# DeltaNet attention and a top-2 expert layer on one Trainium2 core: indirect stores tied to the matmul plan, early tiles in two passes, and another layout of the diagonal copies

## Chip, cores and metric

The kernel runs on one NeuronCore of a Trainium2 chip. The metric is device time in microseconds for the whole kernel. The kernel before took 837.7 us (median of 3 runs, 837.05 to 840.62). All arithmetic is in fp32.

## The reference

```python
# attention: q, k, v are [4, 8, 768, 48], beta is [4, 8, 768]
k_n = k / (norm(k) + 1e-6)
for t in range(768):
    y[:, :, t] = q_t @ state                       # [48] @ [48, 48] per batch and head
    state += beta_t * outer(k_t, v_t - k_t @ state)
x = y laid out as [3072 tokens, 384]
# router and experts: E = 8 experts, D = 384, F = 1024
noisy = x @ w_gate + log1p(exp(x @ w_noise)) * noise
top2, with weights softmax over the two
out[token] += weight_e * relu(x[token] @ w1[e]) @ w2[e]   # for both of its experts
```

## The kernel before

**Attention phase.** The recurrence is done in chunks of 64 tokens. A *unit* is one chunk of two batches (128 partitions) with all 8 heads; four units make a *step* of 128 tokens per batch, and there are six steps (0 to 5), 24 units. For each unit, `products` transposes the keys on TensorE, multiplies them with themselves into two PSUM banks (a `pair` tile), and copies the 32x32 diagonal blocks into an "inverse" tile `t` (four copies of 32 partitions x 256 elements, L658) and the off-diagonal blocks into `at` (L665). `invert` turns a group of one or two steps (`GROUPS`) into inverses on VectorE: a 32x32 transpose (L713), then 30 columns of two operations each (L773, L777), then transposes back (`turn_back`, L793 to L808). `join` builds the 64x64 inverse from the 32x32 ones (L836 copies, L856 and L862 matmuls of 32x32). `recur` scales v on GpSimd (L900), subtracts the state's part on VectorE (L926), solves (L963), and updates the state; `answer` writes the tokens' outputs y (L1044), transposes them and computes the router's logits (L1060). Tiles of y form a ring of three (`NY = 3`), so step 5 uses the tile of step 2.

**Router runs.** `ROUTES` groups the steps in three router runs of two steps. `route` finds the two experts of every token of its 8 units, counts positions with matmuls against a triangular mask, and stores each token's row (384 values of y and 4 of bookkeeping) into the DRAM table `rows_x`, at the slot of each of its two experts: 16 indirect stores of 128 rows per run, issued by GpSimd (`spread`, L396). `cut` raises expert 0's count to a multiple of 128 rows after a step in `EARLY`, so that the tiles before it are complete.

**Early tiles.** `early(s)` computes tiles of expert 0 from rows that are already stored, with weights loaded during the attention phase, in buffers borrowed from the keys of steps 3 and 4 and from q: it loads the rows (L1296), transposes them (L1324), multiplies by w1 (L1350), applies ReLU (L1361), multiplies by w2 (L1374), scales (L1391) and stores them to the output by an indirect DMA (L437). Its jobs have the lowest priority. The kernel before does four tiles at once, after step 3.

**Planner.** All attention-phase work is added to `Jobs`, a list scheduler that runs when the program is built. Every job has an engine, an assumed cost, dependencies (through keys it reads and writes), a due time (`BEGINS`, `ENDS`, `ROUTED`, `STORED`) and perhaps `apart`, a least distance from the last job that has one. `order` simulates the engines: among the jobs of an engine that can begin within `PATIENCE` of the earliest, it takes the one that is due first; a job whose accumulator bank is opened becomes due within `SOON`. The simulated order becomes the order of instructions on each engine; GpSimd's instructions are chained in it. The distance `apart` is not itself in the program: on the chip a store goes as soon as GpSimd reaches it and its inputs are there.

**Expert phase.** After the attention phase the remaining rows of expert 0 are done (`rest`, L1753 and L1765), and experts 1 to 7 follow with a planned sequence of products (L1609).

Of the kernel before, what the change touches and what calls it, by code (L numbers as in the profile page):

```python
# [17 lines left out]
C = 64  # L18
# [1 line left out]
Q = 32  # L20
TILES = 6
MORE = 64
EARLY = {3: (0, 4)}
ROWS = TILES * 128 + MORE
ROW = 384 + 4

# [3 lines left out]
KEYS_AT = [0, 1, 3, 2, 0, 1]  # L30


BEGINS = [37.4, 35.9, 114.1, 181.8]
ENDS = [16.5, 121.4, 125.6, 180.3, 223.6, 257.7]
ROUTED = [145.6, 211.6, 324.9]
STORED = [183.2, 270.8, 339.6]
SOON = 2.12
COLD = [1.6, 1.3, 1.1, 1.1, 1.1, 1.05]
COLD_KEYS = [1.6, 1.6, 1.45, 1.3, 1.1, 1.1]

# [58 lines left out]
class Jobs:  # L99
# [123 lines left out]
                    could[jobs[j].engine].add(j)  # L223
        return sorted(done, key=lambda job: job.start)

    PATIENCE = 0.007

    def run(self, link):

# [11 lines left out]
def kernel(  # L241
# [39 lines left out]
    nc = tc.nc  # L281
# [110 lines left out]
            in_=empty[0:p, None, :].to_broadcast([p, (hi - lo) // p, ROW]),  # L392
        ).ins

    def spread(rows, slot, cleared):
        d = nc.gpsimd.indirect_dma_start(  # L396
            out=rows_x,
            out_offset=bass.IndirectOffsetOnAxis(ap=slot, axis=0),
            in_=rows,
            in_offset=None,  # L400
        ).ins
        tc.declare_no_dep(d, group="spread", reason="no two tokens have the same row")
        tc.add_to_no_dep_group("spread", d)
        for i in cleared:
            tc.add_manual_dep(d, i.name, SYNC, reason="rows cleared before they are written")
        written.append(d)
        return d

# [34 lines left out]
    def deltanet(ictx):  # L443
# [8 lines left out]
        )  # L452
        p_st = psum.tile([128, 2, 512], FP32, name="p_st")
        PE, ACT, DVE, POOL, SP = Jobs.ENGINES

        def bank(size, ahead=False):

# [141 lines left out]
        def turned(n, name, src, slot, to):  # L599

            p = bank(1, True)

            def emit():
                p_t = p.tile.rearrange("p (j t) -> p j t", t=128)
                for j in range(NP):
                    nc.tensor.transpose(p_t[:, j], src(n)[:, 2 * j : 2 * j + 2], ident)

            jobs.add(
                PE, 0.67, emit, reads=halves(name, slot), opens=p,
            )  # L610
            jobs.add(
                ACT, 0.6,
                lambda: nc.scalar.copy(
                    to(n),
                    p.tile.rearrange("p (j t) -> p j t", t=128) if name == "k"
                    else p.tile.rearrange("p (j b t) -> p j b t", b=2, t=C),
                ),
                writes=[(name + "T", slot)], closes=p,
            )

        def by_token(out, lhsT, rhs):

            for j in range(NP):
                for b in range(2):
                    for z in range(2):
                        nc.tensor.matmul(  # L626
                            out[rows_of[b], z, j], lhsT[rows_of[z], j, rows_of[b]],
                            rhs(rows_of[z], j, b), start=(j == 0), stop=(j == NP - 1),
                            skip_group_check=True,
                        )  # L630

        def products(n):

            s, i = divmod(n, US)
            turned(n, "k", kps, slot_of(n), kTs)
            p = bank(2, s > 0)
            jobs.add(  # L640
                PE, 0.69,
                lambda: by_token(
                    two_banks(p, C), kTs(n), lambda z, j, b: kTs(n)[z, j, rows_of[b]]
                ),
                reads=[("kT", slot_of(n))], opens=p,
            )
            _, held_in, half = place_of[s]
            gd = inverses[held_in][:, half].rearrange(
                "p i (u j z) -> p u z j i", u=US, z=2
            )[:, i]  # L650
            for x, lo in enumerate(range(0, 128, Q)):
                rows, cols = slice(lo, lo + Q), slice(lo % C, lo % C + Q)
                on, copy = (DVE, nc.vector.tensor_copy) if s == 0 and x % 2 else (
                    ACT, nc.scalar.copy
                )
                jobs.add(
                    on, 0.38,
                    lambda rows=rows, cols=cols, copy=copy: copy(  # L658
                        gd[rows], two_banks(p, C)[rows, :, :, cols]
                    ),  # L660
                    reads=[("free", held_in, half)], writes=[("gd", held_in, half, i, lo)],
                    uses=p,
                )
            jobs.add(
                ACT, 0.38, lambda: nc.scalar.copy(ats(n), two_banks(p, C)[:, :, :, Q:C]),  # L665
                writes=[("at", slot_of(n))], closes=p,
            )
# [148 lines left out]
        def join(units):  # L816
# [24 lines left out]
            for n, m in zip([*units, None], [None, *units]):  # L841
# [10 lines left out]
                def products_of(n=n, m=m, p_x=p_x):  # L852
                    for h in range(H):
                        for up, dn in pairs:
                            if n is not None:
                                nc.tensor.matmul(  # L856
                                    p_x()[dn, h], ats(n)[up, h % 2, h // 2],
                                    part_of(tbs, n)[up, h], start=(h == 0),
                                    stop=(h == H - 1), skip_group_check=True,
                                )  # L860
                            if m is not None:
                                nc.tensor.matmul(  # L862
                                    p_x()[up, h], xs(m)[dn, h], w64s(m)[dn, h, Q:C],
                                    start=(h == 0), stop=(h == H - 1),
                                    skip_group_check=True,
                                )
# [22 lines left out]
        def recur(n):  # L889
# [50 lines left out]
            if c:  # L940
                p_y = bank(2)

                def of_state():
                    for j in range(NP):
                        for b in range(2):
                            for y in range(2):
                                nc.tensor.matmul(
                                    two_banks(p_y, D)[rows_of[b], y, j],
                                    qss(n)[rows_of[y], j, b, 0:C],
                                    qss(n)[rows_of[y], j, b, C : C + D],  # L950
                                    start=(j == 0), stop=False, skip_group_check=True,
                                )

                jobs.add(
                    PE, 0.68, of_state, reads=[("qT", n % NQ), ("st", n % NQ)],
                    writes=[("of_state", z)], opens=p_y,
                )
            p_u = bank(1)

            def solve():  # L960
                for h in range(H):
                    for b in rows_of:
                        nc.tensor.matmul(  # L963
                            per_head(p_u)[b, h], w64[b, h], v_n[b, h],
                            start=(h == 0), stop=(h == H - 1), skip_group_check=True,
                        )
# [14 lines left out]
            def gather_state():  # L981
                for j in range(NP):
                    for y in range(2):
                        for b in range(2):
                            nc.tensor.matmul(
                                kept[rows_of[y], b, j],
                                kp[rows_of[b], 2 * j + y], u_n[rows_of[b], 2 * j + y],
                                start=(n == 0 and j == 0), stop=(j == NP - 1),
# [14 lines left out]
        def answer(n, p_y):  # L1003
# [11 lines left out]
            def of_chunk():  # L1015
                for j in range(NP):
                    for y in range(2):
                        for b in rows_of:
                            nc.tensor.matmul(  # L1019
                                two_banks(p_y, D)[b, y, j], qk[b, y, j], u_n[b, 2 * j + y],  # L1020
                                start=(c == 0 and j == 0), stop=(j == NP - 1),
                                skip_group_check=True,
# [2 lines left out]
            def turn():  # L1025
                for t in range(KT):
                    cols = slice(t * 128, (t + 1) * 128)
                    nc.tensor.transpose(p_xt.tile[:, cols], y_n[:, cols], ident)  # L1028

            def multiply():  # L1030
                p_l = p_xt.tile[:, KT * 128 : KT * 128 + 2 * E]
                for do in range(KT):
                    nc.tensor.matmul(  # L1033
                        p_l, xTs(n)[:, do], router["wgn"][:, do],
                        start=(do == 0), stop=(do == KT - 1),
                    )
# [44 lines left out]
        def route(g):  # L1081
# [62 lines left out]

            def count_earlier():
                p_at = p.tile[:, 0 : units * E].rearrange("p (u e) -> p u e", e=E)
                nc.tensor.matmul(p_at, mask_u, taken, start=True, stop=False)
                for i in range(1, units):
                    nc.tensor.matmul(
                        p_at[:, i:], ones, taken[:, 0 : units - i],  # L1150
                        start=False, stop=False, skip_group_check=True,
                    )
                nc.tensor.matmul(
                    p_at, ones, before[:, None, :].to_broadcast([128, units, E]),
                    start=False, stop=True,
                )
# [76 lines left out]
            for x in range(units):  # L1233
                of, i = first_s + x // US, x % US
                for to in slot:
# [2 lines left out]
                        lambda x=x, of=of, i=i, to=to: [spread(  # L1238
                            ys(of)[:, i], to[:, x : x + 1],
                            [y for name in clears for y in cleared[name]],  # L1240
                        )],
                        reads=[("slot", g % 2), ("of_y", of % NY), ("y", of % NY, i), *clears],
                        writes=[("rows", of, i, to is slot[1])], lands=2.0, moves=0.7,
                        due=STORED[g], apart=4.5 / steps * paced,
                    )

        def cut(s, rows):
# [4 lines left out]
            def skip():  # L1252
# [7 lines left out]
                )  # L1260

            jobs.add(
                PE, 0.4, lambda: nc.tensor.matmul(p.tile[:, 0:1], ones, before[:, 0:1]),
                reads=["before"], opens=p,
            )
            jobs.add(DVE, 0.4, skip, writes=["before"], closes=p,
# [733 lines left out]
```

## Time and profile before

| | |
|---|---|
| median of 3 runs | 837.7 us |
| the profiled execution's own time | 836.19 us |
| its span, first to last instruction | 834.4 us |
| mean granted clock of TensorE | 0.935 |
| TensorE (PE) matmuls busy | 731.2 us, 88% of the span |
| VectorE (DVE) busy | 555.3 us, 67% |
| ScalarE (ACT) busy | 335.5 us, 40% |
| GpSimd (POOL) busy | 363.8 us, 44% |

Times in the profile count from the first instruction. L396 is line 396 of the kernel; PE, DVE, ACT, POOL and SP are the five engines, PEld is TensorE's loading of weights. In a timeline row the first number is the start, the second how long the merged instructions took; in brackets stands how long the engine was idle before and what ended that. "issue" means that the engine waited for nothing that the profile shows.

### The profile page before, as it was taken

The numbers are of one execution on the slowest core, as the hardware profiler recorded it, in microseconds if no ns is written. First come the engines' busy times: TensorE is split into PE (matmuls) and PEld (weight loads), VectorE is DVE, ScalarE is ACT, GpSimd is POOL, SyncE is SP. The second block draws the span as 40 slices with busy tenths as digits, with TensorE's granted clock in tenths as the row PEclk, the third lists the DMA queues.
The fourth block names the chain that finished last, engine by engine and source line by source line (L and its number), as shares of the span: only waits on it lengthen the run. The fifth ranks groups of instructions, "written<-read, shape, count | busy, mean of one in ns | idle before, by whom it ended". The sixth has DMA issues, their size and how long they took to land.

```text
span 834.4 us, 20583 instructions
## 1 busy us (share of the span) xinstructions
PE 731.2 (88%) x8550; PEld 562.3 (67%) x8550; DVE 555.3 (67%) x1130; ACT 335.5 (40%) x732; POOL 363.8 (44%) x375
## 2 busy tenths in 40 slices
PE   4677778784788678999999999999999999999994
PEld 3456667673677557746558859759669678587593
DVE  5867969990786302205879678688688597796751
ACT  4788689463765225411152051150340430521500
POOL 2111101125300440074457478577675784884511
PEclk9999958985898769999999999999999999999998
DMA  3769855414631331436640921824616407401201
GB/s 58 142 122 324 186 159 118 116 23 137 180 91 39 101 103 52 152 135 139 139 150 1 255 74 40 233 57 87 206 36 174 145 6 196 133 7 54 60 30 33
DMA packets 142215, 93.68 MB, mean 112 GB/s; under 512 B 115868, under 2 KB 134585, under 8 KB 141088
## 3 DMA queue, kind: packets, MB, share of 16 engines
q1 hardware_dynamic: 130448, 64.54, 31.1%
q0 software_dynamic: 9552, 27.33, 9.9%
q8 instruction: 69, 1.13, 0.6%
q10 hardware_dynamic: 2112, 0.39, 0.3%
q14 instruction: 34, 0.28, 0.1%
HBM read 58.82 MB, written 34.81 MB: 112 GB/s over the span
## 4 chain that ended last, share of the span: by engine, by line
PE 53%; issue 5%; POOL 2%; ACT 0%; POOLq 0%; ACTq 0%
PE inner L1609 25%; PE outer L1609 15%; PE pair L1350 3%; PE pair L1374 2%; PE inner L1732 2%; PE inner L1753 2%; PE outer L1765 1%; POOL out_dram L437 1%; POOL sums L428 1%; PE single L1033 1%; PE pair L1019 1%; POOL t_w L1582 0%; PE single L963 0%; PE single L1028 0%; PE pair L626 0%
## 5 line engine op out<-in xcount | busy, mean ns | idle before, releaser
L1692 ACT ACTIVATE hT<-inner 128x416 f32<-128x416 f32 x105 | 54.3, 517 | 256.8 <-PE inner L1609 248.4
L1686 DVE TENSOR_TENSOR hT<-hT,inner 128x416 f32<-128x416 f32 x182 | 105.1, 586 | 45.4 <-PE inner L1609 34.5
L437 POOL DMA_INDIRECT out_dram<-sums,index x52 | 52.9, 1018 | 114.0 <-DVE sums L1512 97.5
L900 POOL TENSOR_TENSOR v<-v,norms 128x384 f32<-128x384 f32 x24 | 21.8, 914 | 164.8 <-DMA v<-in_v_dram 50.3
L1609 PE MATMUL inner<-s_x,w1e 128*128 128x416 f32 x196 | 78.8, 512 | 0.0
L1512 DVE SCALAR_TENSOR_TENSOR sums<-outer,gate,sums 128x192 f32<-128x192 f32 (+1 forms) x113 | 45.8, 415 | 36.1 <-PE outer L1609 35.0
L1681 ACT ACTIVATE hT<-hT 128x416 f32<-128x416 f32 x112 | 60.7, 548 | 21.8 <-DVE hT L1686 13.6
L428 POOL DMA_INDIRECT sums<-out_dram,index x49 | 51.8, 1057 | 19.1 <-issue 11.8
L926 DVE TENSOR_TENSOR v<-v,pair 128x384 f32<-128x384 f32 x22 | 12.1, 552 | 70.9 <-PE pair L626 39.8
L1609 PEld LDWEIGHTS inner<-s_x,w1e 128*128 128x128 f32 x196 | 36.9, 190 | 31.6 <-issue 27.7
L1609 PE MATMUL outer<-t_w,hT 128*128 128x192 f32 x336 | 58.0, 326 | 0.0
L658 ACT COPY t<-pair 32x256 f32<-32x256 f32 x88 | 51.9, 590 | 15.0 <-PE pair L626 9.0
L773 DVE TENSOR_TENSOR part<-t 128x168 f32<-128x168 f32 (+28 forms) x120 | 55.4, 461 | 3.7
L777 DVE TENSOR_TENSOR t<-t,part 128x168 f32<-128x168 f32 (+28 forms) x120 | 54.3, 452 | 4.1
L1609 PE MATMUL inner<-s_x,s_w 128*128 128x416 f32 x140 | 56.9, 512 | 0.0
L396 POOL DMA_INDIRECT rows_x<-y,slot x48 | 48.1, 1002 | 18.9 <-issue 12.4
L1609 PE MATMUL inner<-xe,w1e 128*128 128x416 f32 x140 | 55.8, 513 | 0.0
L1609 PEld LDWEIGHTS outer<-t_w,hT 128*128 128x128 f32 x336 | 55.2, 190 | 0.0
L1566 POOL TENSOR_TENSOR w1e<-w1e 128x256 f32<-128x256 f32 x54 | 51.4, 961 | 2.0
L1609 PE MATMUL outer<-w2e,hT 128*128 128x192 f32 x280 | 50.1, 326 | 0.0
L1609 PEld LDWEIGHTS outer<-w2e,hT 128*128 128x128 f32 x280 | 46.5, 190 | 2.2 <-issue 2.2
L1609 PEld LDWEIGHTS inner<-s_x,s_w 128*128 128x128 f32 x140 | 26.6, 190 | 22.3 <-issue 22.1
(215 smaller groups left out, 1576.0 us busy)
## 6 DMA issues: line engine op xcount, KB each, us to landing
w2e<-in_moe_w_dram SPq DMA_DIRECT2D x8, 1536.0 KB
w1e<-in_moe_w_dram SPq DMA_DIRECT2D x8, 1536.0 KB
xq<-rows_x SPq DMA_DIRECT2D x28, 312.0 KB
rows_x<-empty SPq DMA_DIRECT2D x8, 776.0 KB
v<-in_v_dram SPq DMA_DIRECT2D x48, 96.0 KB
qp<-in_q_dram SPq DMA_DIRECT2D x48, 96.0 KB
out_dram<-empty SPq DMA_DIRECT2D x4, 1152.0 KB
rows_x<-empty SPq DMA_DIRECT2D x8, 485.0 KB
```

The lines of the kernel that those rows point to most:

```text
L396: d = nc.gpsimd.indirect_dma_start(out=rows_x, out_offset=bass.IndirectOffsetOnAxis(ap=slot, axis=0), in_=rows, in_offset=None,).ins
L428: nc.gpsimd.indirect_dma_start(out=got, out_offset=None, in_=out, in_offset=bass.IndirectOffsetOnAxis(ap=index, axis=0), bounds_check=N - ...
L437: nc.gpsimd.indirect_dma_start(out=out, out_offset=bass.IndirectOffsetOnAxis(ap=index, axis=0), in_=got, in_offset=None, bounds_check=N - ...
L658: lambda rows=rows, cols=cols, copy=copy: copy(gd[rows], two_banks(p, C)[rows, :, :, cols]),
L773: v_.tensor_tensor(out=part, in0=factor.to_broadcast(shape), in1=row.to_broadcast(shape), op=ALU.mult,)
L777: v_.tensor_tensor(out=block, in0=block, in1=part, op=ALU.add)
L1512: nc.vector.scalar_tensor_tensor(out=got, in0=p, scalar=gate, in1=got, op0=ALU.mult, op1=ALU.add)
L1566: engine.tensor_tensor(out=block(to), in0=block(x), in1=block(y), op=ALU.add if sign == "+" else ALU.subtract,)
L1609: nc.tensor.matmul(p, lhsT, rhs, start=opens and i == 0, stop=i == len(products) - 1, skip_group_check=True,)
L1681: nc.scalar.activation(h, h, ACTF.Relu)
L1686: nc.vector.tensor_tensor(out=h, in0=h, in1=p, op=ALU.add if sign > 0 else ALU.subtract)
L1692: nc.scalar.mul(h, p, float(sign))
```

## The change

Four things change, and the numbers that steer the planner with them.

1. `spread` gets an argument `behind`. For the first two router runs (`paced`) it is the last TensorE instruction that has been emitted, in planned order, before the store; the store waits for it on a semaphore. To know it, all matmuls and transposes of the attention phase go through small wrappers that record the instruction. The distance `apart` of these stores is 3.3 instead of 4.5 / 2.
2. `EARLY` becomes two entries: tiles 0 and 1 after step 1, tiles 2 and 3 after step 3. `cut` and `early` run once for each.
3. The diagonal copies keep their 32 x 256 elements, but in the order i, j, z instead of z, j, i: the destination is written in runs of eight neighbours, and the source is read with z (the PSUM bank) innermost.
4. `BEGINS`, `ENDS`, `ROUTED`, `STORED`, `SOON` and `PATIENCE` have other values.

```diff
-EARLY = {3: (0, 4)}
+EARLY = {1: (0, 2), 3: (2, 4)}
...
-BEGINS = [37.4, 35.9, 114.1, 181.8]
-ENDS = [16.5, 121.4, 125.6, 180.3, 223.6, 257.7]
-ROUTED = [145.6, 211.6, 324.9]
-STORED = [183.2, 270.8, 339.6]
-SOON = 2.12
+BEGINS = [-21.2, 37.9, 119.9, 189.3]
+ENDS = [24.7, 114.5, 135.1, 205.4, 199.0, 287.8]
+ROUTED = [156.2, 218.8, 313.8]
+STORED = [190.0, 267.2, 353.1]
+SOON = 5.29
+SPACED = 3.3
...
-    PATIENCE = 0.007
+    PATIENCE = 0.036
...
-    def spread(rows, slot, cleared):
+    def spread(rows, slot, cleared, behind):
...
+        if behind is not None:
+            tc.add_manual_dep(d, behind.name, SYNC, reason="not faster than the products")
...
+        latest = [None]
+
+        def matmul(*x, **y):
+            latest[0] = nc.tensor.matmul(*x, **y).ins
+
+        def transpose(*x, **y):
+            latest[0] = nc.tensor.transpose(*x, **y).ins
...
             gd = inverses[held_in][:, half].rearrange(
-                "p i (u j z) -> p u z j i", u=US, z=2
+                "p i (u j z) -> p u i j z", u=US, z=2
             )[:, i]
...
-                        gd[rows], two_banks(p, C)[rows, :, :, cols]
+                        gd[rows],
+                        two_banks(p, C)[rows, :, :, cols].rearrange("p z j i -> p i j z"),
...
                             [y for name in clears for y in cleared[name]],
+                            latest[0] if paced else None,
...
-                        due=STORED[g], apart=4.5 / steps * paced,
+                        due=STORED[g], apart=SPACED * paced,
```

## Rows read from the trace of the kernel before

**Rows 1.** Busy time by stretch: us, PE, PEld, DVE, ACT, POOL, granted clock, DMA share, GB/s

```profile
186.30:206.30 20.00, 7.55 (x103) 5.54 (x104) 0.64 (x1) 6.96 (x15) 13.46 (x14) 0.50 0.40 139
240.00:260.00 20.00, 17.53 (x412) 15.54 (x411) 18.11 (x42) 11.35 (x31) 2.73 (x3) 0.96 0.22 43
280.60:300.60 20.00, 8.77 (x113) 5.10 (x105) 1.62 (x5) 0.92 (x2) 14.50 (x15) 0.63 0.43 151
302.00:346.00 44.00, 40.39 (x1156) 36.59 (x1154) 6.94 (x22) 22.40 (x61) 3.67 (x4) 0.95 0.28 90
```

**Rows 2.** Timeline of POOL: indirect stores of the first two router runs

```profile
186.29 1.72 POOL L396 DMA_INDIRECT rows_x<-y,slot  x1 [0.51 <-POOL y L1227]
...
202.33 0.96 POOL L396 DMA_INDIRECT rows_x<-y,slot  x1 [0.30 <-issue]
...
217.84 1.73 POOL L396 DMA_INDIRECT rows_x<-y,slot  x1 [0.16 <-issue]
...
220.61 1.04 POOL L396 DMA_INDIRECT rows_x<-y,slot  x1 [0.17 <-issue]
...
228.58 1.00 POOL L396 DMA_INDIRECT rows_x<-y,slot  x1 [0.16 <-issue]
...
280.67 1.02 POOL L396 DMA_INDIRECT rows_x<-y,slot  x1 [2.76 <-DVE r_count L1175]
...
298.06 0.97 POOL L396 DMA_INDIRECT rows_x<-y,slot  x1 [0.30 <-issue]
...
309.97 1.00 POOL L396 DMA_INDIRECT rows_x<-y,slot  x1 [0.15 <-issue]
...
312.00 1.01 POOL L396 DMA_INDIRECT rows_x<-y,slot  x1 [0.17 <-issue]
```

**Rows 3.** Busy time by stretch, within the two bursts of stores

```profile
190.40:205.40 15.00, 4.12 (x44) 2.81 (x44) 0.00 (x0) 2.68 (x5) 9.84 (x11) 0.50 0.40 152
281.60:290.70 9.10, 1.92 (x22) 1.33 (x21) 1.16 (x2) 0.58 (x1) 7.08 (x9) 0.73 0.36 134
290.70:300.90 10.20, 5.86 (x53) 2.92 (x54) 0.29 (x2) 0.00 (x0) 6.50 (x7) 0.50 0.52 174
```

**Rows 4.** Timeline of SP and PE near stores that stand alone

```profile
216.26 0.39 SPq L1443 DMA_DIRECT2D w2e<-in_moe_w_dram  x1
...
225.78 0.21 PE L862 MATMUL single<-w,x 32*32 32x32 f32 x1 [3.38 <-issue]
...
311.26 0.20 PE L856 MATMUL single<-tb,at 32*32 32x32 f32 x1 [0.46 <-issue]
...
312.78 1.36 PE L626 MATMUL pair<-qs,kT 64*64 64x112 f32 x32
```

**Rows 5.** Timeline of ACT: the first y copy of step 5

```profile
320.22 0.48 ACT L1044 COPY y<-pair 128x384 f32<-128x384 f32 x1
```

**Rows 6.** Groups by line and shape: three copies of ACT

```profile
L658 ACT COPY t<-pair 32x256 f32<-32x256 f32 x88 | 51.9, 590 | 15.0 <-PE pair L626 9.0 <-DVE t L658 2.8 <-remote 2.4
L836 ACT COPY w<-tt 32x256 f32<-32x256 f32 x88 | 35.4, 402 | 7.5 <-DVE tt L808 4.5 <-DVE r_den L1167 1.6
L665 ACT COPY at<-pair 128x256 f32<-128x256 f32 x20 | 7.4, 372 | 2.2 <-DVE t L658 2.0
```

**Rows 7.** Line L713: what its engine (DVE) idled for, us and times

```profile
  ACT t L658: 10.0, 4
```

**Rows 8.** The chain that ended last, in order of time: start, us, what

```profile
354.25 15.51 PE pair L1350 x36
369.76 20.64 PE pair L1374 x64
...
416.69 3.59 PE inner L1609 x10
```

**Rows 9.** Line L1350: weight loads, ns min/median/max

```profile
L1350 PEld LDWEIGHTS pair<-kT,w1e x32: 186/190/192, 346.8 to 367.9; 128*128 128x128 f32 x32
```

**Rows 10.** Timeline of DVE: the last sums that expert 1 needs

```profile
410.91 1.08 DVE L1573 TENSOR_TENSOR s_x<-s_x,xe 128x416 f32<-128x416 f32 x2
```

More of the change, by code (lines that the diff above doesn't have):

```diff
@@ L605, in emit @@
                 for j in range(NP):
-                    nc.tensor.transpose(p_t[:, j], src(n)[:, 2 * j : 2 * j + 2], ident)
+                    transpose(p_t[:, j], src(n)[:, 2 * j : 2 * j + 2], ident)
             jobs.add(
@@ L625, in by_token @@
                     for z in range(2):
-                        nc.tensor.matmul(
+                        matmul(
                             out[rows_of[b], z, j], lhsT[rows_of[z], j, rows_of[b]],
@@ L855, in products_of @@
                             if n is not None:
-                                nc.tensor.matmul(
+                                matmul(
                                     p_x()[dn, h], ats(n)[up, h % 2, h // 2],
@@ L861, in products_of @@
                             if m is not None:
-                                nc.tensor.matmul(
+                                matmul(
                                     p_x()[up, h], xs(m)[dn, h], w64s(m)[dn, h, Q:C],
@@ L946, in of_state @@
                             for y in range(2):
-                                nc.tensor.matmul(
+                                matmul(
                                     two_banks(p_y, D)[rows_of[b], y, j],
@@ L962, in solve @@
                     for b in rows_of:
-                        nc.tensor.matmul(
+                        matmul(
                             per_head(p_u)[b, h], w64[b, h], v_n[b, h],
@@ L984, in gather_state @@
                         for b in range(2):
-                            nc.tensor.matmul(
+                            matmul(
                                 kept[rows_of[y], b, j],
@@ L1018, in of_chunk @@
                         for b in rows_of:
-                            nc.tensor.matmul(
+                            matmul(
                                 two_banks(p_y, D)[b, y, j], qk[b, y, j], u_n[b, 2 * j + y],
@@ L1027, in turn @@
                     cols = slice(t * 128, (t + 1) * 128)
-                    nc.tensor.transpose(p_xt.tile[:, cols], y_n[:, cols], ident)
+                    transpose(p_xt.tile[:, cols], y_n[:, cols], ident)
             def multiply():
@@ L1032, in multiply @@
                 for do in range(KT):
-                    nc.tensor.matmul(
+                    matmul(
                         p_l, xTs(n)[:, do], router["wgn"][:, do],
@@ L1146, in count_earlier @@
                 p_at = p.tile[:, 0 : units * E].rearrange("p (u e) -> p u e", e=E)
-                nc.tensor.matmul(p_at, mask_u, taken, start=True, stop=False)
+                matmul(p_at, mask_u, taken, start=True, stop=False)
                 for i in range(1, units):
-                    nc.tensor.matmul(
+                    matmul(
                         p_at[:, i:], ones, taken[:, 0 : units - i],
@@ L1152, in count_earlier @@
                     )
-                nc.tensor.matmul(
+                matmul(
                     p_at, ones, before[:, None, :].to_broadcast([128, units, E]),
@@ L1262, in cut @@
             jobs.add(
-                PE, 0.4, lambda: nc.tensor.matmul(p.tile[:, 0:1], ones, before[:, 0:1]),
+                PE, 0.4, lambda: matmul(p.tile[:, 0:1], ones, before[:, 0:1]),
                 reads=["before"], opens=p,
```

## Prediction

> **What bounds the kernel now.** I read the page first: PE is busy 88% of the span and over nine tenths in every slice from the seventeenth on, while slices 1 to 16, the attention phase, stand near seven tenths. The eight experts after it are limited by PE, and the diff doesn't touch them, so the change can only win or lose before about 417 us, where expert 1's first product starts [rows 8].
>
> Then the stretches view. In an ordinary stretch of the attention phase (240 to 260 us) PE is busy 17.5 us of 20 and DVE 18.1. [...]
>
> How much is lost? Inside the first burst, 190.4 to 205.4 us, PE finishes 44 matmuls; inside the second, 281.6 to 300.9, 22 and 53 [rows 3]. The last stretch of the phase runs 1156 matmuls in 40.4 us, 0.035 us each [rows 1]. At that rate 44 take 1.5 us and 75 take 2.6 us (I add 0.9 us for four full-size transposes among them). So 15.0 - 1.5 = 13.5 us and 19.3 - 3.5 = 15.8 us are lost: 29.3 us for 27 stores, 1.09 us per store. The waits name no engine in these gaps ("issue"), ACT and DVE stand too, and the next inversion can't begin. I take the loss as wholly on the path.
>
> **Spacing the stores (the main edit).** Each of the 32 stores of the first two router runs now waits for the latest PE run planned before it, and stands 3.3 planner microseconds from the last instead of 2.25. No instruction is removed. What does a store cost that stands alone? The trace has five: 217.84, 220.61, 228.58, 309.97 and 312.00 [rows 2]. After the first and the third I see no gap. After 309.97 PE has gaps that add up to about 0.46 us, and the product of 32 matmuls after 312.00 takes 1.36 us, 0.24 over 32 times 0.035. Between 222.4 and 225.8 PE stands for 3.38 us, after the store at 220.61 but also in the middle of the 1.5 MB load of w2e issued at 216.26 [rows 4]. So a spaced store costs 0.14 us (0.70 over five) if that stall belongs to the load, and 0.82 us (4.08 over five) if it belongs to the store. I take 0.3, near the lower end, since four of five show little. Then 32 x 0.3 = 9.6 us stand against 29.3 + 0.7 = 30.0 us: a gain of 20 us. By the ends it is 25.5 us and, with the long stall counted on both sides, 33.4 - 26.2 = 7 us. PE idle for less time should also keep the clock up; I count nothing for that.
>
> **What the new wait holds up.** Behind a waiting store on POOL stand the scalings of v (L900), which DVE's subtraction (L926) and PE's solve need; each can come late by the rest of one PE run, about 1 us, and a few of them will be needed at once: +1 us. SP's loads of early rows wait for stores too. The larger matter is the ring of three y tiles: step 5 writes the tile that step 2's eight stores read. Now step 5's first y copy comes at 320.22, 39.5 us after the second run's first store [rows 5]. Without the burst's 15.8 us that is 23.7 us. Eight stores at 3.3 us need 26.4, and about 2 us to land by the planner's own figure, 28.4: a wait of up to 4.7 us. I take +3, together +4 us; the ends are 0 and 8.
>
> **Diagonal copies.** The 96 copies now write runs of eight neighbours instead of single elements 128 bytes apart, and read PSUM alternating between two banks instead of in order. ACT's copy takes 590 ns; a copy of as many elements that writes runs takes 402 ns (L836), and 372 ns from PSUM (L665) [rows 6]. No row reads PSUM in the new order, so a copy costs between 372 and 590 ns. I take 400, nearest to the rows that write runs: 0.19 us less. In step 0 the 16 copies alternate ACT and DVE in one line before the first inversion: 3 us straight from the start. Later, DVE's transposes waited for these copies 10.0 us in all, at four places [rows 7]. Behind them PE and DVE are at nine tenths [rows 1], so what is late next takes most of it back. I take 5 us in all, between 0 and 12.
>
> [...]
>
> **Early tiles in two passes.** Expert 0's first four tiles are done as two and two. PE's first products stream 512 columns in 0.431 us a record (36 in 15.51) [rows 8] with weight loads of 0.190 us hidden beneath [rows 9]; with 256 columns there are twice as many at 0.215 us, still above 0.190, so PE's time is the same, and the second products (64 records, 20.64 us) don't change. Eight more ReLUs on ACT hide under PE. Two things are new. The second pass loads its rows into buffers that the first pass's last products read, so between the passes there are a load, three transposes and copies, some 4.5 us, of which three more product pairs (about 1 us each) cover 3: +1.5 us, at most 6. And the first pass can go into gaps earlier, but its buffers are those of steps 3 and 4, and PE is busy 40.4 of the last 44 us, so at most 3.6 us move, and then DVE's sums bound: they end at 412.0, 4.7 us before PE needs them [rows 8, 10]. I take +1 in all, from -4 to +6. The second padding of expert 0's count costs one matmul and two DVE operations of about 0.15 us. Counted from the reference's inputs, expert 0 still ends at 766 rows, under the 832 of a slice, so the branch for left-over rows stays out.
>
> **The new due times and patience** reorder the attention phase. They add and remove no work, and no row says which order is better: I count 0, and 5 us each way.
>
> **Sum.** -20 (bursts) + 4 (waits) - 5 (copies) + 1 (passes) = -20 us. The profiled execution took 836.2 us with a span of 834.4, so 816 us; the median of the runs is 1.5 us above it: 817.7. I predict 817 us.
>
> **Rivals.**
> *The loss goes with the stores, not with their density.* If a store costs 1.09 us wherever it stands, 32 of them cost as much as before: -5 + 4 + 1 = 0, about 838 us. For it: PE stalled 0.9 us after the second burst's first store. Against it: four of five spaced stores.
> *The pace binds (slower).* The stores follow PE's plan; if PE runs behind, they spread further. Step 5's copies wait 8s + 2 - 23.7 us for a real spacing s. At 3.3 that is 4.7; it eats the remaining gain of 23 us from s = 5.6 us, and at 7 us it is 34 us, so some 849 us. Against it: ordinary stretches keep PE at nine tenths, so the plan isn't far off.
> *The copies gain nothing* because reads replace writes as their limit: 5 us on any case, 822 with the rest as forecast. [...]
> *The order gets worse* than I can see: 5 to 10 us, mixed into the others.
>
> **Chances.** Spaced stores are cheap: 0.66 (of it 0.20 with copies that gain nothing), own range 804 to 828 us. Loss per store stays: 0.20, 828 to 842. Pace binds: 0.10, 836 to 860. Anything else: 0.04. A measurement can tell about 0.5%, 4.2 us. Below 833.5: nearly all of the first and a third of the second, 0.73. Within: 0.12. Above 841.9: 0.15. The range from 803 to 839 holds the first case and most of the second.
>
> **What the profile will show.** Right: the first 32 stores start 3 us or more apart; stretches with stores have over 300 matmuls per 20 us and little "issue"; L658 means about 400 ns; 96 records of 128x256 on L1350; expert 1 starts near 397 us. Wrong: gaps of 0.7 us after every store; L658 still at 590 ns or above; y copies or scalings of v waiting for POOL; PE idle between the two early passes.

## The result and the profile after

The changed kernel took 802.42 us (median of 4 runs, 800.57 to 804.69) beside 837.38 us of the kernel before on the same chip (4 runs): a ratio of 0.9582, with a 95% interval from 0.9539 to 0.9625, 35 us faster. I had forecast 817, from 803 to 839. The profiled execution took 801.79 us with a span of 799.7.

First the stretches of the changed kernel's trace, in the columns of [rows 1]: two in which the first run's stores go, an ordinary one, one with the second run's stores, and the last of the phase, where the early products now stand among the rest.

```profile
176.90:196.90 20.00, 16.65 (x477) 15.18 (x479) 15.03 (x32) 13.31 (x33) 6.32 (x6) 0.76 0.54 155
196.90:216.90 20.00, 15.57 (x533) 13.42 (x531) 16.45 (x29) 14.81 (x36) 7.66 (x8) 0.91 0.72 197
...
240.00:260.00 20.00, 18.84 (x572) 17.09 (x572) 11.98 (x43) 11.86 (x32) 1.27 (x3) 0.80 0.34 72
263.10:283.10 20.00, 17.26 (x689) 15.36 (x689) 3.67 (x8) 10.93 (x27) 7.75 (x9) 1.00 0.34 93
...
302.00:346.00 44.00, 39.66 (x206) 31.29 (x202) 8.13 (x40) 11.82 (x37) 20.65 (x24) 1.00 0.49 175
```

Where [rows 1] had 103 and 113 matmuls in 20 us of stores, there are now 477 and 689, and PE is busy for 16.7 and 17.3 us instead of 7.6 and 8.8. In the second run's stretch the granted clock is 1.00, where it was 0.63.

The stores in POOL's timeline (the first, second and last of each of the two runs, then the first two of the third), which answer to [rows 2]:

```profile
176.92 1.19 POOL L397 DMA_INDIRECT rows_x<-y,slot  x1 [1.06 <-DVE r_count L1187]
181.44 0.96 POOL L397 DMA_INDIRECT rows_x<-y,slot  x1 [3.33 <-PE pair L461]
...
236.92 1.00 POOL L397 DMA_INDIRECT rows_x<-y,slot  x1 [3.07 <-PE single L461]
263.08 1.03 POOL L397 DMA_INDIRECT rows_x<-y,slot  x1 [1.57 <-DVE qk L945]
265.51 0.96 POOL L397 DMA_INDIRECT rows_x<-y,slot  x1 [1.40 <-PE pair L461]
...
307.93 0.96 POOL L397 DMA_INDIRECT rows_x<-y,slot  x1 [0.41 <-PE single L461]
318.44 0.98 POOL L397 DMA_INDIRECT rows_x<-y,slot  x1 [3.06 <-DVE r_count L1187]
319.72 0.96 POOL L397 DMA_INDIRECT rows_x<-y,slot  x1 [0.30 <-issue]
```

Each store of the first two runs now waits for a PE instruction (L461 and L464 are the new wrappers): 16 take 60.0 us from first to last, 4.0 apart on average, the next 16 take 44.9, 3.0 apart. The third run, which has no such wait, goes back to back. In the trace before, 13 of the first 16 start from 186.29 to 202.33 us and 14 of the next 16 from 280.67 to 298.06, most of them 1.27 us apart: the two bursts, 27 of the 32 stores.

The copies by line and shape, which answer to [rows 6] (L669 was L658, L848 was L836, L677 was L665), and what DVE's transposes idled for (L725, once L713, [rows 7]):

```profile
L669 ACT COPY t<-pair 32x256 f32<-32x256 f32 x88 | 32.0, 363 | 11.1 <-PE pair L461 8.1 <-DVE t L669 1.9
L848 ACT COPY w<-tt 32x256 f32<-32x256 f32 x88 | 35.4, 402 | 2.4 <-DVE tt L820 0.8
L677 ACT COPY at<-pair 128x256 f32<-128x256 f32 x20 | 7.5, 373 | 1.7 <-DVE t L669 1.5
```

```profile
L725 DVE STREAM_TRANSPOSE t<-t x6: 1187/1226/1246, 16.6 to 182.7; 128x1024 f32<-128x1024 f32 x6
...
  ACT t L669: 6.1, 3
```

A diagonal copy takes 363 ns instead of 590, and the transposes wait 6.1 us instead of 10.0. The first transpose starts at 16.6 us; before it was 20.08.

The chain that ended last, around the second early pass, answers to [rows 8]:

```profile
331.65 10.63 PE pair L1363 x48
342.27 2.98 issue
345.25 10.59 PE pair L1387 x32
...
382.13 28.09 PE inner L1622 x80
```

Expert 1 starts at 382.13 instead of 416.69, 34.6 us earlier; nothing behind it changed. So the gain lies ahead of it. By the two timelines the first run's first store comes 9.4 us earlier, the second's 17.6 and the third's 37.8; in the early passes 3 us are given back.

### The profile page after: what moved, and what is told of

The parts are those of the page before. It is cut to its first block, busy times and chain, and to the rows that moved or that the text cites. A ratio compares the mean times of both kernels' runs of the same rounds, so it can differ in the third digit from the quotient of the medians.

```text
span 799.7 us, 20716 instructions
## 1 busy us (share of the span) xinstructions
PE 729.0 (91%) x8600; PEld 573.3 (72%) x8600; DVE 560.1 (70%) x1132; ACT 318.7 (40%) x740; POOL 361.3 (45%) x375
## 4 chain that ended last, share of the span: by engine, by line
PE 73%; issue 9%; ACT 6%; DVE 5%; POOL 3%; DMA 2%; SPq 1%; POOLq 0%; DVEq 0%; ACTq 0%
PE inner L1622 26%; PE outer L1622 16%; PE single L461 9%; PE pair L461 8%; PE single L464 4%; PE pair L1363 2%; PE inner L1745 2%; PE p_st L461 2%; PE inner L1766 2%; DVE part L785 2%; DMA kp<-in_k_dram 2%; ACT w L848 1%; PE pair L1387 1%; PE outer L1778 1%; DVE t L789 1%
## 5 line engine op out<-in xcount | busy, mean ns | idle before, releaser
L912 POOL TENSOR_TENSOR v<-v,norms 128x384 f32<-128x384 f32 x24 | 21.5, 896 | 113.0 <-DMA v<-in_v_dram 69.8
L1525 DVE SCALAR_TENSOR_TENSOR sums<-outer,gate,sums 128x192 f32<-128x192 f32 (+1 forms) x113 | 45.9, 416 | 36.1 <-PE outer L1622 34.6
L1694 ACT ACTIVATE hT<-hT 128x416 f32<-128x416 f32 x112 | 60.7, 548 | 21.8 <-DVE hT L1699 13.6
L789 DVE TENSOR_TENSOR t<-t,part 128x168 f32<-128x168 f32 (+28 forms) x120 | 56.4, 470 | 4.1
L1622 PEld LDWEIGHTS inner<-xe,w1e 128*128 128x128 f32 x140 | 26.4, 190 | 20.1 <-issue 19.9
L1622 PE MATMUL outer<-t_w,s_h 128*128 128x192 f32 x224 | 40.6, 329 | 0.0
```

The costliest lines, as they stand in the source:

```text
L789: v_.tensor_tensor(out=block, in0=block, in1=part, op=ALU.add)
L1525: nc.vector.scalar_tensor_tensor(out=got, in0=p, scalar=gate, in1=got, op0=ALU.mult, op1=ALU.add)
L1622: nc.tensor.matmul(p, lhsT, rhs, start=opens and i == 0, stop=i == len(products) - 1, skip_group_check=True,)
L1694: nc.scalar.activation(h, h, ACTF.Relu)
```

## The experiments

The runs fell on chips of two kinds. On one (chips 7 and 8, and the chip of the result above) the kernel before has medians of 837 to 841 us; on the other (chips 1, 2 and 3) 807.6 to 809.3. I call them **first** and **second kind**. Chip 8 was used twice, minutes apart, and was of the first kind both times (840.02 and 841.11 us); every other numbered chip was used once. That the kind belongs to the chip, and not to the moment, rests on chip 8 alone. A gain is worked out from a run's ratio to the kernel before on its own chip, times that kernel's time there; two ratios are only compared within a kind. Ratios have intervals of about 0.004 each way, so a difference of two is known to 5 us or so.

**The wait alone, both ways (first kind).** One kernel is the changed one without the wait:

```diff
-                            latest[0] if paced else None,
+                            None,
```

> The changed kernel, but no store waits for a TensorE run; the planned order is the same on PE, DVE, ACT and SP. Theory (the wait keeps the stores apart, and stores back to back cost about 1 us each): the first 32 stores bunch again, PE has under 200 matmuls per 20 us in such a stretch, and the time goes back by 20 to 30 us, to 822-832 us. Rival (the gain came from the copies and the new order, the wait did little): at most 808 us, with or without bursts.

827.53 us, ratio 0.9857 (0.9819 to 0.9895): 0.0275 above the changed kernel's, 23 us. The bursts are back (two stretches of it, same columns):

```profile
175.50:188.50 13.00, 7.64 (x95) 5.61 (x96) 4.40 (x7) 1.39 (x3) 10.19 (x10) 0.50 0.45 154
269.00:287.00 18.00, 7.30 (x96) 4.30 (x86) 1.45 (x4) 0.64 (x2) 14.15 (x15) 0.60 0.45 154
```

The other is the kernel before, with its order of instructions on every engine, and the wait added (`spread` and the wrappers of the change, but `apart` still 2.25):

```diff
-SPACED = 3.3
+SPACED = 2.25
-EARLY = {1: (0, 2), 3: (2, 4)}
+EARLY = {3: (0, 4)}
```

with the due times, patience and copies of before as well.

> The kernel before, in its own order and with its own copies and spacing of 2.25, with the wait alone. Theory (density): the two bursts go and 20 to 27 us with them, 810-817 us. Rival (a loss per store, wherever it stands, or the gain lies in copies and order): 830 us or more, with gaps of 0.7 us after spaced stores. Second rival (the pace binds): step 5's y copies wait for stores and the time is above 820.

817.47 us, ratio 0.9752 (0.9703 to 0.9801): 21 us faster. Its stretches of stores:

```profile
191.00:211.00 20.00, 16.61 (x438) 14.56 (x437) 9.05 (x17) 17.63 (x41) 9.52 (x11) 0.74 0.50 139
278.30:298.30 20.00, 16.54 (x621) 14.34 (x623) 3.76 (x9) 8.83 (x22) 9.51 (x10) 1.00 0.39 112
```

So the wait is worth 21 to 23 us, whichever kernel it is put in or taken from. The spacing in the plan does little by itself: 3.3 without the wait gives bursts, 2.25 with it gives none (no run changes the spacing alone). Both rivals (the loss per store stays, the pace binds) fall, on this kind of chip: in this trace too what the y copies wait for is PE, 15.9 of the 16.1 us that ACT idled before them.

**The copies alone, both ways (first kind).** The changed kernel with the old order of elements, and the kernel before with the new one:

```diff
-                "p i (u j z) -> p u i j z", u=US, z=2
+                "p i (u j z) -> p u z j i", u=US, z=2
...
-                        two_banks(p, C)[rows, :, :, cols].rearrange("p z j i -> p i j z"),
+                        two_banks(p, C)[rows, :, :, cols],
```

> The changed kernel with the diagonal copies in their old element order (ACT about 590 ns again); order the same. Theory of the prediction: the copies are worth 5 us, so 807 us, of it 3 us before the first inversion of step 0. Rival (they were mis-sized and carry most of the 9.4 us by which the first store comes earlier): 811-815 us. Second rival (what is late next takes it all back): 802-804 us.

> The kernel before with the new diagonal copies alone; order the same, bursts stay. Theory of the prediction: 5 us, so 832 us. Rival (copies worth 9 us): 828 us. Second rival (taken back behind): 836-837 us.

810.44 us, ratio 0.9669 (0.9629 to 0.9709), 0.0087 above the changed kernel's: 7 us. And 826.03 us, ratio 0.9852 (0.9812 to 0.9892): 12 us faster than before. The copies' rows in the one and the other:

```profile
L669 ACT COPY t<-pair 32x256 f32<-32x256 f32 x88 | 52.0, 591 | 11.7 <-PE pair L461 7.9 <-DVE t L669 2.8
```

```profile
L658 ACT COPY t<-pair 32x256 f32<-32x256 f32 x88 | 32.0, 363 | 15.0 <-PE pair L626 8.7 <-remote 3.4 <-DVE t L658 1.9
```

So the copies give 7 to 12 us, not 5. The first difference is uncertain by some 5 us and doesn't exclude 5; the second, 9 to 16 us by its interval, does.

**A surprise: the other kind of chip.** The next four kernels ran on chip 3, where the kernel before takes 809.27 us. First the kernel before with wait and copies (the second kernel above with the new order of elements):

> The kernel before, in its own order, one early pass, spacing 2.25, with the wait and the new copies. If the parts add up (wait alone 21.7 us, copies alone about 12), 804 us, and the new due times, the spacing of 3.3 and the two passes are worth nothing together. If the copies are worth only the 7 us that they gave on the changed kernel, 809 us, and the order and the passes gave the other 6 us.

798.21 us, ratio 0.9855 (0.9815 to 0.9895): a gain of 12 us, where I expected some 30 (804 to 809 us from 838). Against a kernel before of 809 us that expectation can't be judged. The changed kernel with the due times and patience of before:

```diff
-BEGINS = [-21.2, 37.9, 119.9, 189.3]
+BEGINS = [37.4, 35.9, 114.1, 181.8]
...
-    PATIENCE = 0.036
+    PATIENCE = 0.007
```

(and so on for `ENDS`, `ROUTED`, `STORED` and `SOON`)

> The changed kernel with the due times and the patience of before; wait, spacing 3.3, copies and two passes stay. The prediction's 0 for the order: 802-805 us. Rival (the order carries the missing gain): 808 us or more. If the pace binds in this order, step 5's y copies wait for stores and it is above 812.

794.16 us, ratio 0.9825 (0.9781 to 0.9869). Then both kernels without the 32 stores of the first two runs:

```diff
     def spread(rows, slot, cleared, behind):
+        if len(written) + skipped[0] < 32:
+            skipped[0] += 1
+            return None
```

> The changed kernel without the 32 stores of the first two router runs (left out: those rows stay padding, so the experts' results are of other rows, their number is the same); order the same. The prediction's 0.3 us for a spaced store and 4 us of waits: 790-794 us. Rival (a spaced store is free): 801-803 us. A loss per store at any density (1.09 us): 768 us.

> The kernel before without the same 32 stores (left out likewise); order the same. The prediction's 29.3 us of the bursts plus 0.7 to 4 us of five spaced ones: 803-808 us. If the burst's loss is partly covered by other waits behind it, 812-820 us.

791.01 us, ratio 0.9768 (0.9718 to 0.9818), and 802.07 us, ratio 0.9903 (0.9864 to 0.9942). The kernel before without its stores is close to where I expected it, at 802 us (803 to 808), but here the stores had cost only 8 us: the kernel *with* them was 28 us faster on this chip than I knew it.

**Both kernels on one chip of the second kind.** On chip 1 the two kernels ran unaltered, and both also without the 32 stores.

> The changed kernel unaltered, to stand beside the next three on one chip. On a chip where the kernel before takes about 838 us: 802-806 us. On a chip where it takes about 809 us (as in the run without stores): if the gain is that of the bursts, which cost little there, only about 12-16 us, 793-798 us; if the change gains the same everywhere, 775 us.

> The kernel before without the 32 stores of the first two runs (left out), on the chip of this call. If the stores are the whole difference between chips: 800-805 us also where the kernel before takes 838, so that they cost 33-38 us there (the prediction had 30.0). If something else differs between chips: 820 us or more there.

> The changed kernel without the same stores, on the chip of this call. If spaced stores cost the prediction's 0.3 us each, 9-11 us below the changed kernel: about 791 us. If they are free: equal to the changed kernel.

> The kernel before unaltered, for its trace on this chip. Where it takes about 838 us: under 150 matmuls per 20 us in the two bursts. Where it takes about 809 us: if the bursts are what differs, over 250 matmuls per 20 us in them; if they stall the engines alike, the 28 us lie elsewhere, in shorter gaps all over the attention phase.

The kernel before takes 808.64 us here. The changed kernel: 800.98, ratio 0.9905 (0.9871 to 0.9940), a gain of 8 us, not 35. Without stores: before 0.9910 (0.9873 to 0.9947), after 0.9847 (0.9815 to 0.9880). So here the stores cost the kernel before 7.3 us and the changed one 4.7, 0.15 us each (with the 791.01 us of chip 3 in place of this chip's run it would be 11, so the figure is a rough one). The trace of the kernel before on this chip, its stores (the first and last of each burst) and the two stretches:

```profile
186.03 1.71 POOL L396 DMA_INDIRECT rows_x<-y,slot  x1 [0.51 <-POOL y L1227]
...
202.09 0.96 POOL L396 DMA_INDIRECT rows_x<-y,slot  x1 [0.30 <-issue]
...
270.60 1.02 POOL L396 DMA_INDIRECT rows_x<-y,slot  x1 [2.58 <-DVE r_count L1175]
...
287.98 0.97 POOL L396 DMA_INDIRECT rows_x<-y,slot  x1 [0.30 <-issue]
```

```profile
186.00:206.00 20.00, 15.38 (x441) 13.19 (x441) 9.29 (x18) 19.36 (x45) 16.23 (x17) 0.82 0.64 191
270.60:290.60 20.00, 16.86 (x707) 15.25 (x697) 4.93 (x11) 9.71 (x23) 15.97 (x17) 1.00 0.57 173
```

This is the same program with the same bursts: 13 stores from 186.03 to 202.09 here, 13 from 186.29 to 202.33 in [rows 2]. There PE ran 103 matmuls beside them, here 441; in the second burst 113 there, 707 here. So back-to-back stores stall the engines on the one chip and hardly on the other.

**Is it the stores alone, and what are the two passes worth?** These two ran on chip 8, of the first kind (before: 840.02 us).

```diff
-EARLY = {1: (0, 2), 3: (2, 4)}
+EARLY = {3: (0, 4)}
```

> The changed kernel with one early pass of four tiles, as before; due times, wait, spacing and copies stay. The prediction's +1 us for two passes: 1 us less than the changed kernel, whose ratio to the kernel before is 0.958 where that takes 838 us and 0.9905 where it takes 809. Rival (the first pass really goes into gaps and 4 us are gained): 4-6 us more. Rival (the bubble between the passes, 2.6 and 3.0 us in the trace after, is all lost): 4 us less.

> The kernel before without the 32 stores of the first two runs (left out), once more, for the case that this call's chip is one where the kernel before takes about 838 us. If the stores alone make it slower there: 800-805 us, a cost of 33-38 us (the prediction: 30.0). If those chips are slower in other work too: 815 us or more. Where the kernel before takes 809 us: 801 us again.

The kernel before without its stores: 803.16 us, ratio 0.9600 (0.9546 to 0.9653), against 801.26 and 802.07 on chips of the second kind. So the stores are the whole difference between the chips, to within 2 us; on the first kind they cost 33.6 us by the ratio (29 to 38). The changed kernel with one pass: 810.12 us, ratio 0.9643 (0.9603 to 0.9684), 0.0061 above the changed kernel's: two passes are 5 us faster, where I had 1 us slower; the interval reaches down to about nothing. Its PE timeline shows a wait that the first pass fills in the changed kernel, and a stretch at a granted clock of 0.50 after it:

```profile
312.91 0.69 PE L461 MATMUL single<-r_taken,mask_u 128*128 128x64 f32 x2 [6.25 <-DVE r_taken L1110]
...
320.25 3.78 PE L1363 MATMUL pair<-kT,w1e 128*128 128x512 f32 x4 [0.35 <-ACT kT L1349]
```

```profile
312.00:322.00 10.00, 8.68 (x32) 6.85 (x33) 4.36 (x30) 2.62 (x13) 2.88 (x5) 0.50 0.99 355
```

PE waits 6.25 us for the last router run, and the early products begin at 320.25. In the changed kernel they begin at 303.95, among the last logits. The wait is not all of it: the 14 counting matmuls of the last router run, first in the changed kernel, then in the one with a single pass, show what the clock adds behind it (granted 1.00 from 302 to 346 us in the one, 0.50 from 312 to 322 in the other):

```profile
314.65 1.68 PE L461 MATMUL single<-r_taken,ones 128*128 128x56 f32 x14
...
313.39 3.10 PE L461 MATMUL single<-r_taken,ones 128*128 128x56 f32 x14
```

The gap belongs to the new order: no trace with the old one has it.

**Bytes or number of stores?** The kernel before, its 32 stores writing 16 bytes a row instead of 1552:

```diff
-            out=rows_x,
+            out=rows_x if len(written) > 31 else rows_n,
...
-            in_=rows,
+            in_=rows if len(written) > 31 else rows[:, 0:4],
```

> The kernel before, whose 32 stores of the first two runs write 16 bytes a row to another tensor instead of 1552 (left out: the rest of those rows; the experts' results are of other rows). Number, rows and times of the stores as before. Where the kernel before takes about 838 us: if the stall goes with the number of stores and rows, 835-840 us with under 150 matmuls per 20 us in the bursts; if it goes with the bytes written, 803-810 us. Where it takes 809 us: 801-809, which tells little.

> The 32 stores with 16 bytes a row, once more, for a chip where the kernel before takes about 838 us. Stall by number of stores and rows: 835-840 us and bursts with under 150 matmuls per 20 us. Stall by bytes: 803-810 us. On a chip where it takes 809 us: 808-812 us again.

On chip 2, of the second kind, it took 811.72 us, ratio 1.0022 (0.9983 to 1.0062). On chip 8 it took 839.18 us, ratio 1.0001 (0.9965 to 1.0038), and these are its stretches of stores:

```profile
181.50:201.50 20.00, 10.15 (x171) 6.94 (x171) 3.61 (x8) 8.45 (x18) 14.24 (x16) 0.52 0.10 12
...
281.90:301.90 20.00, 5.27 (x95) 3.64 (x87) 1.37 (x4) 0.98 (x2) 14.38 (x15) 0.66 0.03 3
```

The core moves 3 GB/s (last column) in the second burst where [rows 1] had 151, and PE does 95 matmuls where it did 113. In the first burst it does 171, more than the 150 that I named, but the time is the same. So on this chip the time doesn't depend on the bytes (ratio 1.0001), and without the stores it falls to 0.9600 of the kernel before: the stall goes with the stores themselves, their 128 rows or their issue.

**The due times again.** The same kernel as above, on chips 2 and 8.

> The changed kernel with the due times and patience of before, once more: its 0.9825 against the changed kernel's 0.9905 came from two chips. If the old due times are better: where the kernel before takes 809 us again 0.98-0.985; where it takes 838 us 0.945-0.953, 791-798 us, below the changed kernel's 0.958. If the difference was between chips: 0.957-0.960 there.

> The changed kernel with the due times and patience of before. On a chip where the kernel before takes about 838 us: 0.945-0.953 of it if the old due times are the better ones there too, 0.957-0.960 if they are equal. On one where it takes 809 us: 0.980-0.988 again.

796.21 us, ratio 0.9867 (0.9818 to 0.9917), on the second kind, and 802.85 us, ratio 0.9549 (0.9493 to 0.9606), on the first. The changed kernel has 0.9905 and 0.9582 there. All three runs lie below it, by 0.0033 to 0.0080; two of their intervals overlap its own, that of chip 3 ends just under it. So the new due times gain nothing and may cost a few us: with the old ones the kernel beats the kernel before on both kinds, and is level with the changed one or better. Nor do due times, spacing and the two passes together show a gain: on the second kind the kernel before with wait and copies alone stands at 0.9855, the whole change at 0.9905, and on the first kind the wait alone (21 us) and the copies alone (12) already add up to 33 of the 35 us.

## Why the prediction was right or wrong

The direction and the mechanism were right, the size was not: 35 us instead of 20, just past the low end of the range. What failed is the sum, "-20 (bursts) + 4 (waits) - 5 (copies) + 1 (passes)": the three terms beside the bursts were each off in the same direction. By the runs of the first kind, bursts and waits together gave 21 to 23 us instead of 16, the copies 7 to 12 instead of 5, the passes 5 instead of -1, and the order -3 instead of 0: 30 to 37 us, each part uncertain by some 5.

**What the stores cost before** was sized well: 29.3 + 0.7 = 30.0 us forecast, 33.6 (29 to 38) measured by leaving them out. The way to count it, matmuls done in the burst against the rate of a stretch nearby, held. (Two readings beside it were off without weight: PE's gaps after the store at 309.97 are 0.17 and 0.46 us, and the one after the second burst's first store is 0.39, not 0.9.) But I took it for a property of the kernel. It is one of the kernel on some chips: on the second kind the same stores cost 7.3 and 7.8 us, and the forecast of a 20 us gain would have been far too high, for the change gives 8 us there.

**What they cost after** was too dear: 0.3 us each, 9.6, and 4 for the waits, 13.6 us. On the second kind 4.7 us were measured on one chip. On the first no run leaves the spaced stores out. If the two kernels without stores are as far apart there as on chip 1 (0.0063) or chip 3 (0.0135), the changed one without them would stand at 0.9600 less that, 0.9465 to 0.9537; with them it is at 0.9582, 4 to 10 us more, and the intervals add some 5. So the 0.3 us of a store may stand, and little is left for the waits. The net of the bursts, 20 - 4 = 16 us, was 21 to 23 when the wait alone was added or removed. The step of it that failed was the ring of y tiles, +3 us: I let step 5's first copy wait for all eight stores of step 2. The timelines of ACT and POOL say otherwise:

```profile
282.62 0.48 ACT L1056 COPY y<-pair 128x384 f32<-128x384 f32 x1
```

```profile
282.90 0.96 POOL L397 DMA_INDIRECT rows_x<-y,slot  x1 [2.86 <-ACT w L886]
```

The copy is step 5's first, 19.5 us after the second run's first store, and the store is the seventh of the eight. The copy needs only two of them, because it writes one unit's quarter of the tile, and two stores read that quarter. What the engine of the 24 y copies (ACT) idled for before them names PE and never POOL:

```profile
  PE pair L461: 10.3, 11
  PE single L464: 1.1, 1
  issue: 0.4, 1
```

Nor does any engine wait for the scalings of v (L912) in the trace, my other +1.

**The copies**, 590 to 400 ns and 5 us: they take 363, and are worth 7 to 12 us. The 3 us straight from the start were right (3.5, the first transpose). What was wrong is that "what is late next takes most of it back": the first store of the kernel before with new copies comes 7.4 us earlier, at 178.88 instead of 186.29. The rival by which the reads would take the writes' place as the limit is dead: the new read alternates between two banks with every element, and ACT's 363 ns are the least of the three copies. That such a read could hold the copy at 590 ns was my guess, and no run shows it.

**Two passes**, +1: it was -5 (0 to -10), just beyond the -4 to +6 that I gave. The step that failed is "PE is busy 40.4 of the last 44 us, so at most 3.6 us move": that is the kernel before. With the new order the last router run leaves PE a gap of 6.25 us and a clock of 0.50 behind it (312 to 322 us), and the first pass stands in it. So what the passes give hangs on the order, and I had priced the two apart. With the old due times the two passes and the spacing of 3.3 show 2 us on chip 3 (0.9855 without them, 0.9825 with), less than the noise. The bubble between the passes is there, but not for the buffers that I named. The second load of rows is made to wait for every store that stands before it in the program, and in the chain that ended last it begins when the third run's sixth store has landed:

```profile
324.78 2.58 DMA rows_x<-y,slot
...
327.63 2.38 DMA kp<-rows_x
```

PE then waits 1.0 us, transposes from 330.14 to 331.3, and stands 2.98 us before the second products of this pass.

**The new order**, 0 with 5 us each way: it cost 3 us on the first kind (0.0033), and 3 and 6 on the second, each within the noise of 5 or just outside; 0 was off by no more than that. For the clock I counted nothing, and its mean over the span shows no gain: 0.935 before, 0.926 after.

**The third run, and the bubble of 2.98 us.** The third run's stores (318.44 to 342.69) have no wait. The trace of the changed kernel on the first kind has these waits of ACT's ReLU (from 318 to 350 us) and of PE (300 to 358):

```profile
ACT kp L1374 <- remote: 7.8, 2, 4.6
```

```profile
PE pair L1387 <- issue: 3.0, 1, 3.0
```

Neither is in its trace on chip 1. The two other traces of this order on the first kind with two passes (without the wait, and with the old copies) have the wait of PE too, 3.8 us in each. That fits a stall of ACT by that burst, worth 3 us on the first kind; no run spaces those stores, so it is not shown.

**The signs.** Matmuls per stretch, the copies (363 ns, below the 400) and the 96 records on the early line came as named. The pace of 3 us or more came only on average: the second run's stores come as near as 1.4 us (306.56 and 307.93), since the distance is still only the plan's. Expert 1 starts at 382, not at 397. Of the signs of being wrong one came, PE idle between the early passes, as told above. The two rivals that reached 838 and more fell with the wait alone.

**What stays open** is why some chips stall. In the bursts of both kinds most stores take 0.96 to 0.97 us and start 1.27 apart, and with 16 bytes a row the ratio is 1.0022 and 1.0001; which step of a store holds up the engines, and what differs between the chips, no run here tells. The trace of the kernel before has one more clue. Inside the first burst PE doesn't stand still: its small matmuls come in groups about 0.7 us apart, each after an idle time that no engine ends.

```profile
191.15 0.24 PE L856 MATMUL single<-tb,at 32*32 32x32 f32 x1 [0.41 <-issue]
...
191.87 0.24 PE L856 MATMUL single<-tb,at 32*32 32x32 f32 x1 [0.40 <-issue]
...
192.60 0.24 PE L862 MATMUL single<-w,x 32*32 32x32 f32 x1 [0.39 <-issue]
```

What hands them out at that pace, no run shows.

## What to carry to other kernels

This kernel's 32 indirect stores, 27 of them back to back, cost 33.6 us on one chip, 1.05 each, and 7.3 and 7.8 on two others, 0.23 and 0.24 each. Tying each store to the matmul planned before it took away what the two kinds of chip differed by: 802.42 and 800.98 us, where the kernel before was 29 us apart. It gave 21 to 23 us where the stores had cost 33.6, and no y copy and no engine that uses v was seen to wait for the stores that it held back. Look at a stretch where several engines stand and the waits name none on a second chip before pricing it, and when a trace has such a stall, price the waits that a cure adds at the grain of the dependency (here a quarter of a tile), not of the buffer.

## What the runs showed of the hardware

- Beside a burst of indirect stores of 128 rows, most of them 1.27 us apart, PE did 103 and 113 matmuls of the small sizes in 20 us on a chip of the first kind, and 441 and 707 on chip 1, of the second. All 32 stores cost 33.6 us on chip 8 against 7.3 and 7.8 on chips 1 and 3.
- With 16 bytes a row instead of 1552 the time on chip 8 is the same (ratio 1.0001).
- ACT copies 32x256 fp32 elements from PSUM in 363 ns when it writes runs of eight and reads two banks in turn, and in 590 when it reads in order and writes single elements 128 bytes apart.
